# Token rows permuted over the partitions in a fused adaLN, dilated-attention and SwiGLU block

## The chip, the cores and the metric

The kernel runs on one core of a Trainium2 chip. The core has five engines with instruction queues of their own: TensorE (PE, with its weight loads listed as PEld), VectorE (DVE), ScalarE (ACT), GpSimd (POOL) and SyncE (SP), and sixteen DMA engines that all queues share. The metric is the device time of one execution in microseconds (us). A profiled execution gives, beside its time, a trace of every instruction and DMA; the span of that trace is a little shorter than the time.

## The reference

All tensors are bf16; S = 2048 tokens, D = 512, H = 32 heads of 16, F = 1792.

```python
mod = (silu(c) @ w_mod)                  # c is one row; six vectors of D: sa, ca, ga, sb, cb, gb
h = layernorm(x) * (1 + ca) + sa         # LN1
q, k, v = split(h @ wqkv)                # 32 heads of 16
# token s attends to the 8 tokens s, s-2, s-4, ..., s-14 (those >= 0)
logits[s, w] = q[s] . k[s - 2*w] / 4
o[s] = sum_w softmax(logits)[s, w] * v[s - 2*w]
x = x + ga * (o @ wo)
h = layernorm(x) * (1 + cb) + sb         # LN2
x = x + gb * ((silu(h @ w1) * (h @ w3)) @ w2)
```

## The kernel before

The tokens are 16 tiles of 128 rows, one token a partition. Weights and x stay in SBUF.

**LN1 and projections.** Five groups of tiles ([0,1], [2,3], [4..7], [8..11], [12..15]). DVE takes the statistics (L534, L535), POOL the inverse root (L539, L541), DVE normalises (L546). The normalised tile is then turned so that features lie on the partitions: for groups 0 to 2 on PE with an identity matrix (L606), moved out of PSUM by ACT or DVE with the modulation's scale and shift (L614, L621); for the groups named in `DMA_T[0]` (3 and 4) by a DMA transpose that SP issues, and ACT scales in place (L591). PE projects q and k with features on the partitions (L661), which ACT evicts to `q` and `kT` (L670, L671), and v with tokens on the partitions (L681), which ACT evicts (L691) and SP stores to a scratch buffer in DRAM, `v_scratch`. That buffer has 16 zero rows in front.

**Attention, tile by tile.** DVE multiplies q with eight shifted copies of k in one instruction (L712). PE sums each head's 16 features with a block matrix E (L722): 16 matmuls of 256 columns with a 128x32 stationary operand, in four column groups that run side by side; tile 0 gets a mask first (L719). DVE takes the maximum, subtracts (L734, L739), ACT takes the exponential for two tiles (L752), DVE sums, inverts, scales (L764, L766, L767), PE turns the weights so that (token, shift) pairs lie on the partitions (L777), and ACT evicts them (L781). The values arrive from `v_scratch` in that layout: the partition is a pair (one of 16 token runs, shift w), and the free dimension is eight tokens of 512 features. Before the change this is four DMAs a tile, each with 2 KB runs (two consecutive tokens):

```python
for q in range(4):
    p.dma(vv[:, 2*q:2*q+2, :], AP(v_dram, (PAD + T*P + 32*q)*D, [[2*D, 16], [-DIL*D, W], [1, 2*D]]), ...)
```

DVE multiplies weights and values (L797), PE sums over the shifts with an indicator (L825), ACT evicts (L831), a DMA transpose turns the result, PE applies `wo` (L837), which DVE has scaled by ga, and DVE adds to x (L841).

**LN2 and FFN.** Six groups ([0,1], [2,3], [4..7], [8..11], [12,13], [14,15]). POOL and ACT normalise (L556, L560, L567, L571), the tile is turned on PE (groups 0 and 1) or by DMA (`DMA_T[1]`), and for 14 feature blocks PE computes gate and up (L853), ACT the SiLU (L859), DVE the product (L862). PE applies w2 (L891; in halves for tiles 14 and 15, L879), DVE adds x (L901), and SP stores.

**What sets the order.** The program is a list of operations with a cost, read and write sets, and buffer slots. Two written lists, `ORDER` (one position for each operation) and `SLOTS` (buffer numbers), come from a search against a cost model, in which `packet_ns` and the constants in `Program.dma` price the DMAs. Each engine runs its operations strictly in the order of that list and waits on semaphores, so a waiting instruction holds everything behind it on its engine; SP's queue holds nearly all DMA issues. `GATES` adds waits in front of some weight loads.

Of the kernel before, what the change touches and what calls it, by code (L numbers as in the profile page):

```python
# [10 lines left out]
P = 128  # L11
# [58 lines left out]
def packet_ns(size):  # L70
    return {256: 18, 512: 27, 768: 36, 1024: 48, 2048: 92, 3072: 138}[size]


class Program:
# [41 lines left out]
    def dma(self, out, in_, key, packets, r=(), w=(), part=(), after=(), eng="sp", cost=450, group=None, transpose=False,  # L116
            store=False, again=False, lat=None):
        nc = self.nc

        def fn(e):  # L120
            a = out() if callable(out) else out
            b = in_() if callable(in_) else in_
            with nc.allow_non_contiguous_dma(reason="layout"):
                return e.dma_start(a, b, transpose=True) if transpose else e.dma_start(a, b)  # L124

        n, size = packets
        each = -(-n // 16)
        ns = 600 if transpose else each * (126 if again else packet_ns(size))
        o = self.op(eng, fn, cost, key, r=r, w=w, part=part, after=after, dma=(each, ns, *(lat if lat else (900, 200) if store else (900, 500) if transpose else (1300, 600))))
        if group is not None:  # L130
            group.append(o)
            o.group = group
        return o
# [116 lines left out]
BEFORE = -1e9 / P  # L250
# [17 lines left out]
DMA_T = ((3, 4), (2, 3, 4, 5))  # L268
AC_OLD = ()
# [3 lines left out]
def _build(p, A_x, A_wqkv, A_wo, B_w1, B_w3, B_w2, c, w_mod, out):  # L273
# [4 lines left out]
    x_view = x2d.rearrange("(t p) d -> p t d", p=P)  # L278
# [26 lines left out]
    ident = sb([P, P], bf, "ident")  # L305
    E_sb = sb([P, KT, H], bf, "E")
# [53 lines left out]
    def held(pool, items):  # L360

        vals = []
        for i, item in enumerate(items):
# [13 lines left out]
                                           pattern=[[-1, P]], channel_multiplier=1), 300, k, w=[vident])  # L377
    p.op("pool", lambda e: e.memset(cst[:, 0:1], EPS), 80, k, part=[vcst])
# [13 lines left out]
    for y in range(2):  # L392
        p.op("dve", lambda e, y=y: e.tensor_copy(bass.AP(ind2, 33 * y, [[64, P], [2, 16]]), ind[:]), 150, k, r=[vind], w=[vind2])
    p.op("pool", lambda e: e.memset(before[:], 0.0), 250, k, w=[vbefore])
    p.op("pool", lambda e: e.affine_select(out=before[:], in_=before[:], compare_op=ALU.is_ge, fill=BEFORE, base=0,
                                           pattern=[[-DIL, W], [1, 2], [2, 16]], channel_multiplier=0), 400, k, w=[vbefore])
# [10 lines left out]
    p.dma(x_sb[:, 0:2, :], x_view[:, 0:2, :], ("load", 1), (256, 1024), w=vx[0:2])  # L407
    p.dma(wm_s[0][:], wm_view[:, :, 0:1024], ("load", 2), (512, 2048), w=[vwms[0]])
    p.dma(x_sb[:, 2:4, :], x_view[:, 2:4, :], ("load", 27), (256, 1024), w=vx[2:4])
# [4 lines left out]
    for g in range(1, 4):  # L414
        p.dma(x_sb[:, 4 * g:4 * g + 4, :], x_view[:, 4 * g:4 * g + 4, :], ("load", 5 + g), (512, 1024), w=vx[4 * g:4 * g + 4])
# [163 lines left out]
    def ln_T(which, gi, vns):  # L579
        vh = Val("h", hpool)  # L580
        vh.pieces = [Val(f"h_{ft}") for ft in range(KT)] if not which and not gi else None
# [15 lines left out]
        for half in range(2):  # L597
            k = ("tr", (2 * gi + half) + (2 * len(LN1) if which else 0))
            vt = Val("ps_tr", psum)
            for tt in range(n):  # L600
                def tr(e, tt=tt, vt=vt, half=half):
                    b = bank(vt).bitcast(bf)
                    for j in range(2):
                        col = j * 512 + tt * P
                        ft = 2 * half + j
                        ins = e.transpose(b[:, col:col + P], vns[tt].at[:, ft * P:(ft + 1) * P], ident[:])  # L606
                    return ins

                p.op("pe", tr, 114, k, r=[vns[tt], vident], part=[vt])
# [35 lines left out]
    def proj_qk(gi, Ts, kind, vh):  # L645
# [7 lines left out]
        for f0 in range(0, KT, m):  # L653
# [13 lines left out]
            def ev(e, f0=f0, vp=vp):  # L667
                src = bank(vp)[:, 0:m * n].rearrange("p (j n) -> p j n", j=m)
# [4 lines left out]
            p.op("act", ev, c_act(m * n), k, r=[vp], part=[dstv])  # L673

    def proj_v(T, tt, vh):
# [19 lines left out]
        p.dma(v_dram[PAD + T * P:PAD + (T + 1) * P, :], lambda: vt.at[:], k, (128, 1024), r=[vt], w=[vd], cost=400, store=True)  # L695
# [5 lines left out]
    def logits(Ts):  # L701

        vl = Val("ps_l", psum)
        for i, T in enumerate(Ts):
# [11 lines left out]
            def red(e, i=i, T=T, vp=vp):  # L716
                c0 = vl.at * 512 + i * W * 32
                if T == 0:
                    e.matmul(PALL[0:32, c0:c0 + W * 32], ones[:, 0:32], before[:], start=True, stop=False, tile_position=(0, 0))  # L719
                for ft in range(KT):  # L720
                    for q in range(4):
                        ins = e.matmul(PALL[32 * q:32 * q + 32, c0:c0 + W * 32], E_sb[:, ft, :], bass.AP(vp.at, ft * P + 32 * q, [[W * KT * P, P], [KT * P, W], [1, 2], [2, 16]]),  # L722
                                       start=(ft == 0 and (T > 0 or q > 0)), stop=(ft == KT - 1), tile_position=(0, 32 * q))
# [61 lines left out]
    def values(T, i, val):  # L785

        vv = Val("vsh", vshpool)
        loads = []
        for q in range(4):
            p.dma(lambda q=q: vv.at[:, 2 * q:2 * q + 2, :],  # L790
                  bass.AP(v_dram, (PAD + T * P + 32 * q) * D, [[2 * D, 16], [-DIL * D, W], [1, 2 * D]]), ("vl", T), (128, 2048),
                  r=[vv_dram[T]] + ([vv_dram[T - 1]] if T else [vvpad]), part=[vv], group=loads, cost=640, again=True)
# [10 lines left out]
        if T in AC_OLD:  # L803
            def acc(e):
                b = bank(vo)
                for g in range(8):
                    for ft in range(KT):
                        ins = e.matmul(b[:, ft * P + 16 * g:ft * P + 16 * g + 16], vv.at[:, g, ft * P:(ft + 1) * P], ind[:],
                                       start=True, stop=True)
                return ins  # L810

            p.op("pe", acc, C_ACC, ("ac", T), r=[vv, vind], w=[vo])
    
            def ev(e):
                dst = bass.AP(vt.at, 0, [[KT * P, P], [32, 4 * KT], [1, 2], [2, 16]])
                src = bass.AP(PALL, bank(vo).offset, [[8 * 512, P], [32, 4 * KT], [16, 2], [1, 16]])
                return e.activation(dst, src, ACT.Copy)

            p.op("act", ev, c_act(512), ("ac", T), r=[vo], w=[vt])
        else:  # L820
            def acc2(e):
                c0 = vo.at * 512
                for y in range(2):
                    for q in range(4):
                        ins = e.matmul(PALL[32 * q:32 * q + 32, c0:c0 + 512], ind2[:, y, :], vv.at[:, 2 * q + y, :], start=(y == 0),  # L825
                                       stop=(y == 1), tile_position=(0, 32 * q))
                return ins

            p.op("pe", acc2, C_RED, ("ac", T), r=[vv, vind2], w=[vo], tiled=True)
            va = Val("ac", acpool)  # L830
            p.op("act", lambda e: e.activation(va.at[:], bank(vo), ACT.Copy), c_act(512), ("ac", T), r=[vo], w=[va])  # L831
            p.dma(lambda: vt.at[:], lambda: va.at[:], ("ot", T), (128, 1024), r=[va], w=[vt], cost=1270, transpose=True)
# [66 lines left out]
    def store(T, c0, n, vz):  # L899
# [3 lines left out]
        finals.append(p.dma(out2d[T * P:(T + 1) * P, c0:c0 + n], lambda: vo.at[:, 0:n], ("zo", T), (128, 2 * n), r=[vo], cost=400, store=True))  # L903
# [47 lines left out]
GATES = [-1, -1, -1, -1, -1, -1, -1, -1, -1, 1, -1, -1, -1, -1, -1, 1, -1, -1, 2, -1]  # L951
ORDER = [
    19, 18, 5, 0, 1, 3, 8, 55, 20, 14, 64, 15, 22, 67, 4, 2, 21, 66, 9, 65, 26, 58, 10, 23, 56, 24, 62, 50, 25, 85, 60, 29, 57, 86, 51,
    27, 61, 16, 87, 52, 88, 80, 63, 53, 59, 34, 81, 89, 28, 54, 82, 91, 83, 68, 84, 95, 70, 69, 74, 72, 75, 94, 36, 90, 77, 96, 93, 73,
    71, 113, 97, 103, 92, 133, 123, 152, 79, 138, 78, 153, 128, 150, 108, 76, 144, 151, 190, 154, 155, 191, 182, 129, 139, 124, 109,
    183, 180, 145, 104, 134, 114, 125, 181, 105, 11, 157, 140, 110, 156, 146, 135, 188, 184, 115, 185, 126, 147, 111, 127, 189, 141,
    192, 148, 106, 130, 186, 136, 163, 162, 142, 187, 116, 131, 159, 193, 158, 107, 143, 340, 112, 6, 164, 149, 98, 99, 194, 100, 118,
    37, 165, 101, 341, 119, 195, 120, 121, 35, 161, 17, 198, 199, 197, 236, 204, 160, 203, 202, 196, 205, 137, 237, 172, 246, 122, 117,
    206, 247, 168, 290, 200, 291, 342, 238, 173, 170, 207, 239, 298, 240, 166, 241, 379, 102, 299, 244, 132, 7, 171, 174, 32, 245, 201,
    243, 12, 248, 177, 253, 242, 169, 296, 249, 167, 348, 297, 250, 224, 368, 349, 300, 251, 369, 358, 212, 255, 220, 213, 254, 222,  # L960
    356, 216, 223, 252, 178, 210, 225, 46, 343, 359, 288, 301, 371, 217, 357, 289, 303, 175, 179, 214, 302, 380, 211, 360, 292, 293,
    378, 230, 258, 361, 176, 259, 295, 350, 226, 294, 233, 370, 390, 215, 362, 345, 307, 256, 208, 351, 381, 363, 227, 209, 31, 364, 33,
    257, 218, 365, 228, 262, 388, 231, 229, 30, 366, 285, 263, 232, 367, 306, 270, 221, 372, 219, 260, 305, 279, 261, 304, 286, 13, 266,
    382, 271, 280, 47, 268, 287, 267, 373, 234, 389, 346, 344, 400, 374, 383, 391, 375, 384, 420, 272, 309, 235, 276, 310, 281, 401,
    311, 282, 347, 392, 385, 308, 264, 393, 277, 402, 316, 422, 269, 265, 403, 274, 283, 413, 394, 376, 411, 395, 410, 421, 396, 423,
    412, 397, 386, 39, 377, 278, 398, 41, 320, 387, 399, 284, 275, 611, 334, 404, 613, 331, 317, 612, 324, 321, 424, 614, 405, 273, 615,
# [79 lines left out]
```

## Time and profile before

| | us |
|---|---|
| three runs | 245.97, 275.12, 1143.53 (median 275.12) |
| profiled execution, its time | 243.86 |
| profiled execution, its span | 242.0 |
| PE busy | 232.3 |
| DVE busy | 180.0 |
| ACT busy | 135.6 |
| POOL busy | 23.2 |
| mean share of the 16 DMA engines (queue q1) | 61.6% |

The three runs lie far apart, and the profiled execution is close to the lowest of them. TensorE ran at full granted clock throughout. The costliest groups by line are the gate and up matmuls (L853, 102.7 us), the w2 matmuls (L891, 43.3), the q and k projections (L661, 31.6) on PE, and the query-key and weight-value products (L712, 36.4; L797, 29.7 and 6.9 for two names of the buffer) on DVE. The DMA issues of the page by number: 64 V loads of 256 KB (names sb_vsh and sb_vshx), 36 transposes, 18 output stores, 16 V stores, 20 late weight loads, five loads of x.

In such a page, a row of a stage or a group gives busy time and how many instructions; "idle before" is the time that the engine stood still in front of them and what ended it. A chain of waits is followed back from the last instruction, at each step to what released it.

### The profile page before, as it was taken

How to read it: one execution, taken by the hardware profiler on the slowest of the kernel's cores; microseconds unless marked ns; L12 is line 12 of the kernel's file. 1: busy time of each engine (PE TensorE's matmuls, PEld its weight loads, DVE VectorE, ACT ScalarE, POOL GpSimd, SP SyncE). 2: the span in 40 equal slices, each digit the busy share in tenths (PEclk: the TensorE clock that was granted, in tenths of full speed). 3: DMA queues.
4: the chain of work that ended last, by engine and by line, in shares of the span. 5: the costliest groups of instructions: out<-in, count | busy, mean ns of one | idle time of the engine just before them, and what ended most of it. 6: DMA issues, size and time to landing. Idle time of an engine off the chain costs nothing.

```text
span 242.0 us, 4516 instructions
## 1 busy us (share of the span) xinstructions
PE 232.3 (96%) x1778; PEld 135.8 (56%) x1803; DVE 180.0 (74%) x278; ACT 135.6 (56%) x269; POOL 23.2 (10%) x66
## 2 busy tenths in 40 slices
PE   7999999979899999999999999999999999999995
PEld 2667454434368777674444454444444555768864
DVE  4689999968899999999999999928443611433532
ACT  2178498757979743794774479262476334314200
POOL 4144110002003000040000012000010100000000
PEclk9999999999999999999999999999999999999999
DMA  6998999899999879698292189674031010010004
GB/s 219 385 355 286 172 257 264 132 253 261 305 323 285 228 199 237 148 270 176 71 242 80 33 172 240 141 174 131 3 103 27 0 24 22 23 45 0 3 0 130
DMA packets 45756, 38.84 MB, mean 160 GB/s; under 512 B 21656, under 2 KB 36520, under 8 KB 45736
## 3 DMA queue, kind: packets, MB, share of 16 engines
q1 hardware_dynamic: 45728, 38.56, 61.6%
q8 instruction: 14, 0.23, 0.4%
q14 instruction: 6, 0.05, 0.1%
q10 hardware_dynamic: 8, 0.00, 0.0%
HBM read 29.62 MB, written 4.21 MB: 140 GB/s over the span
## 4 chain that ended last, share of the span: by engine, by line
PE 73%; DVE 13%; DMA 6%; SPq 3%; ACT 1%; issue 1%; POOL 0%; DVEq 0%; ACTq 0%
PE pall L853 39%; PE pall L891 17%; DVE sb_pq L712 5%; PE pall L837 4%; DMA sb_vsh<-v_scratch_dram 3%; SPq L124 3%; PE pall L825 2%; PE pall L497 2%; PE pall L879 2%; DVE sb_vsh L797 2%; DVE sb_st L534 2%; DMA sb_wo<-in_A_wo_dram 2%; DMA v_scratch_dram<-sb_v 2%; PE pall L722 2%; PE pall L661 1%
## 5 line engine op out<-in xcount | busy, mean ns | idle before, releaser
L853 PE MATMUL pall<-sb_h,sb_w 128*128 128x256 bf16 (+1 forms) x665 | 102.7, 307 | 0.9 <-ACT sb_sg L859 0.4
L853 PEld LDWEIGHTS pall<-sb_h,sb_w 128*128 128x128 bf16 x672 | 64.6, 98 | 36.0 <-issue 1.3
L859 ACT ACTIVATE sb_sg<-pall 128x256 bf16<-128x256 f32 (+1 forms) x84 | 35.1, 455 | 49.1 <-PE pall L853 44.4
L862 DVE TENSOR_TENSOR sb_hh<-sb_sg,pall 128x256 bf16<-128x256 bf16 (+1 forms) x84 | 39.6, 506 | 29.0 <-PE pall L853 27.1
L891 PE MATMUL pall<-sb_w,sb_hh 128*128 128x512 bf16 x187 | 43.3, 379 | 0.5
L712 DVE TENSOR_TENSOR sb_pq<-sb_q,sb_kT 128x4096 bf16<-128x4096 bf16 x16 | 36.4, 2285 | 0.0
L661 PE MATMUL pall<-sb_h,sb_wqkv 128*128 128x512 bf16 (+1 forms) x156 | 31.6, 335 | 1.6 <-ACT sb_h L591 0.7
L797 DVE TENSOR_TENSOR sb_vsh<-sb_vsh,sb_al 128x4096 bf16<-128x4096 bf16 x13 | 29.7, 2288 | 3.2 <-DMA sb_vsh<-v_scratch_dram 1.9
L891 PEld LDWEIGHTS pall<-sb_w,sb_hh 128*128 128x128 bf16 x196 | 19.0, 98 | 20.7 <-issue 0.4
L591 ACT ACTIVATE sb_h<-sb_h,sb_modc 128x512 bf16<-128x512 bf16 (+1 forms) x24 | 16.4, 737 | 15.7 <-DMA sb_h<-sb_xn 15.6
L661 PEld LDWEIGHTS pall<-sb_h,sb_wqkv 128*128 128x128 bf16 x160 | 14.7, 98 | 13.6 <-ACT sb_h L591 1.3
L901 DVE TENSOR_TENSOR sb_o<-pall,sb_x 128x512 bf16<-128x512 f32 (+1 forms) x18 | 11.1, 628 | 14.4 <-PE pall L891 11.7
L681 PE MATMUL pall<-sb_wqkv,sb_h 128*128 128x512 bf16 x63 | 16.5, 379 | 0.1
L837 PE MATMUL pall<-sb_wo,sb_ot 128*128 128x512 bf16 x61 | 15.6, 379 | 1.0 <-DMA sb_ot<-sb_ac 0.8
L556 POOL TENSOR_SCALAR sb_nm<-sb_sx 128x2 f32<-128x2 f32 x8 | 2.7, 332 | 129.0 <-DVE sb_x L841 129.0
L614 ACT ACTIVATE sb_h<-pall,sb_modc 128x256 bf16<-128x256 bf16 (+1 forms) x18 | 10.3, 629 | 7.8 <-PE pall L606 7.8
L831 ACT ACTIVATE sb_ac<-pall 128x512 bf16<-128x512 f32 x16 | 9.4, 601 | 7.6 <-PE pall L825 7.5
L571 ACT ACTIVATE sb_xn<-sb_x,sb_nb,sb_rs 128x512 bf16<-128x512 bf16 x16 | 12.6, 810 | 1.6 <-POOL sb_nb L569 1.4
L841 DVE SCALAR_TENSOR_TENSOR sb_x<-pall,sb_x 128x512 bf16<-128x512 f32 x16 | 10.7, 686 | 3.6 <-PE pall L837 3.6
L534 DVE BATCH_NORM_STATS2 sb_st<-sb_x 128x6 f32<-128x512 bf16 x16 | 10.7, 669 | 2.2 <-DMA sb_x<-in_A_x_dram 2.2
L671 ACT ACTIVATE sb_kT<-pall 128x512 bf16<-128x512 f32 (+1 forms) x18 | 9.6, 566 | 4.6 <-PE pall L661 4.6
L560 ACT ACTIVATE sb_xn<-sb_x,sb_nm 128x512 bf16<-128x512 bf16 x16 | 11.6, 725 | 0.7 <-POOL sb_nm L556 0.6
(86 smaller groups left out, 202.1 us busy)
## 6 DMA issues: line engine op xcount, KB each, us to landing
sb_vsh<-v_scratch_dram SPq DMA_DIRECT2D x52, 256.0 KB, 4.5
sb_w<-in_B_w_dram SPq DMA_DIRECT2D x6, 512.0 KB, 5.0
sb_vshx<-v_scratch_dram SPq DMA_DIRECT2D x12, 256.0 KB, 5.0
sb_w<-in_B_w_dram SPq DMA_DIRECT2D x6, 384.0 KB, 4.4
v_scratch_dram<-sb_v SPq DMA_DIRECT2D x16, 128.0 KB, 4.1
out_dram<-sb_o SPq DMA_DIRECT2D x14, 128.0 KB, 1.8
sb_wqkv<-in_A_wqkv_dram SPq DMA_DIRECT2D x4, 384.0 KB, 7.7
sb_x<-in_A_x_dram SPq DMA_DIRECT2D x3, 512.0 KB, 7.8
```

Source lines behind the costliest of these rows:

```text
L534: o = p.op("dve", lambda e, T=T: e.bn_stats(st[:, T, :], x_sb[:, T, :]), 595, ("st", T), r=[vx[T]], w=[vs])
L571: p.op("act", lambda e, vn=vn, T=T: e.activation(vn.at[:], x_sb[:, T, :], ACT.Identity, bias=nb[:, T, :], scale=rs[:, NT + T, :]), c_act(5 ...
L591: return e.activation(vh.at[:, ft, 0:n * P], vh.at[:, ft, 0:n * P], ACT.Identity, bias=modc[:, 8 * which + ft:8 * which + ft + 1], scale=m ...
L661: ins = e.matmul(bank(vp)[:, j * n:(j + 1) * n], wqkv[:, t, col:col + P], vh.at[:, t, 0:n], start=(t == ORDER[0]), stop=(t == ORDER[-1]))
L681: ins = e.matmul(bank(vp), vh.at[:, t, tt * P:(tt + 1) * P], wqkv[:, t, 2 * D:3 * D], start=(t == ORDER[0]), stop=(t == ORDER[-1]))
L712: return e.tensor_tensor(vp.at[:], in0, in1, ALU.mult)
L797: return e.tensor_tensor(v_w, v_w, a_w, ALU.mult)
L837: ins = e.matmul(bank(vy), vt.at[:, ft, :], wo[:, ft, :], start=(ft == 0), stop=(ft == KT - 1))
L853: ins = e.matmul(bank(vp)[:, 0:n], wt[:, t, fi * P:(fi + 1) * P], vh.at[:, t, 0:n], start=(t == 0), stop=(t == KT - 1))
L859: p.op("act", lambda e: e.activation(vt.at[:, 0:n], bank(vgp)[:, 0:n], ACT.Silu), c_act(n), k, r=[vgp], w=[vt], table="silu")
L862: p.op("dve", lambda e: e.tensor_tensor(vh_.at[:, 0:n], vt.at[:, 0:n], bank(vup)[:, 0:n], ALU.mult), c_dve(n), k, r=[vt, vup], w=[vh_])
L891: ins = e.matmul(bank(vz), vhh[fi].at[:, tt * P:(tt + 1) * P], w2[:, fi, :], start=(fi == 0), stop=(fi == NF - 1))
```

## The change

Partition p of a tile holds another token than before: token row g + 8x of the tile lies on partition 16g + x (g from 0 to 7, x from 0 to 15). The loads of x and the stores of the output go through a row pattern with that order; x is loaded tile by tile, 15 loads on SP's queue and one (tile 1) on ACT's.

```diff
-    x_view = x2d.rearrange("(t p) d -> p t d", p=P)
+    def rows(t, T, c0=0, w=D):
+        return bass.AP(t.tensor, t.offset + T * P * D + c0, [[D, 8], [8 * D, 16], [1, w]])
...
-    p.dma(x_sb[:, 0:2, :], x_view[:, 0:2, :], ("load", 1), (256, 1024), w=vx[0:2])
+    def load_x(T, eng="sp"):
+        p.dma(x_sb[:, T, :], rows(x2d, T), ("load", 40 + T), (128, 1024), w=[vx[T]], eng=eng)
+    load_x(0)
+    load_x(1, "act")
...
-        finals.append(p.dma(out2d[T * P:(T + 1) * P, c0:c0 + n], lambda: vo.at[:, 0:n], ("zo", T), (128, 2 * n), r=[vo], cost=400, store=True))
+        finals.append(p.dma(rows(out2d, T, c0, n), lambda: vo.at[:, 0:n], ("zo", T), (128, 2 * n), r=[vo], cost=400, store=True))
```

q, k and the scratch buffer of v keep the tokens' natural order. Where LN1 turns a tile on PE, a permutation matrix (two new POOL operations) takes the identity's place. Where a DMA turns it (`vh.turned`, groups 3 and 4), the evictions of q and k write in permuted columns, and the V store goes through the row pattern.

```diff
+                        ins = e.transpose(b[:, col:col + P], vns[tt].at[:, ft * P:(ft + 1) * P],
+                                          ident[:] if which else perm[:].rearrange("p x g -> p (x g)"))
...
+                if vh.turned:
+                    src = bass.AP(PALL, bank(vp).offset, [[8 * 512, P], [P, n // P], [16, 8], [1, 16]])
+                    to = [[P, n // P], [1, 8], [8, 16]]
+                    if kind == 0:
+                        return e.activation(bass.AP(dstv.at, f0 * 512 + at0, [[KT * 512, P]] + to), src, ACT.Copy, scale=SCALE)
+                    return e.activation(bass.AP(kT, f0 * (PAD + S) + PAD + 512 * cch + at0, [[KT * (PAD + S), P]] + to), src, ACT.Copy)
...
+        p.dma(bass.AP(v_dram, (PAD + T * P) * D, [[D, 8], [8 * D, 16], [1, D]]) if vh.turned else v_dram[PAD + T * P:PAD + (T + 1) * P, :], ...)
```

The logit reduction picks its tokens in steps of eight (16 bytes) instead of two (4 bytes), so that the eight tokens of a partition in the V layout are consecutive rows of the scratch buffer, and V is one load of 1 MB with 8 KB runs a tile. The mask of tile 0 becomes four matmuls with one contraction row each.

```diff
-                    e.matmul(PALL[0:32, c0:c0 + W * 32], ones[:, 0:32], before[:], start=True, stop=False, tile_position=(0, 0))
+                    for q in range(4):
+                        e.matmul(PALL[32 * q:32 * q + 32, c0:c0 + W * 32], ones[32 * q:32 * q + 1, 0:32], before[32 * q:32 * q + 1], start=True,
+                                 stop=False, tile_position=(32 * q, 32 * q))
...
-  bass.AP(vp.at, ft * P + 32 * q, [[W * KT * P, P], [KT * P, W], [1, 2], [2, 16]])
+  bass.AP(vp.at, ft * P + 2 * q, [[W * KT * P, P], [KT * P, W], [1, 2], [8, 16]])
...
-        for q in range(4):
-            p.dma(lambda q=q: vv.at[:, 2 * q:2 * q + 2, :],
-                  bass.AP(v_dram, (PAD + T * P + 32 * q) * D, [[2 * D, 16], [-DIL * D, W], [1, 2 * D]]), ("vl", T), (128, 2048),
+        p.dma(lambda: vv.at[:], bass.AP(v_dram, (PAD + T * P) * D, [[8 * D, 16], [-DIL * D, W], [1, 8 * D]]), ("vl", T), (128, 8192),
```

LN2's group 1 (tiles 2 and 3) is turned by DMA instead of on PE. The cost model's DMA constants change, and `ORDER`, `SLOTS` and `GATES` are replaced by the result of a new search; an unused branch (`AC_OLD`) goes.

```diff
-DMA_T = ((3, 4), (2, 3, 4, 5))
-AC_OLD = ()
+DMA_T = ((3, 4), (1, 2, 3, 4, 5))
...
-    return {256: 18, 512: 27, 768: 36, 1024: 48, 2048: 92, 3072: 138}[size]
+    return {256: 18, 512: 27, 768: 36, 1024: 47, 2048: 92, 3072: 127}[size]
...
-        ns = 600 if transpose else each * (126 if again else packet_ns(size))
+        ns = 650 if transpose else each * (400 if again else packet_ns(size))
```

In the new order SP's queue begins x0, x2, w_mod's first half, wqkv (third block), x3, x5, two blocks of wqkv, x4, the last block, x7, x6, the two gate parts of w_mod, x9, x8, the zero rows, x10, x11, part of wo, two V stores, x12, x15, x14. On DVE the statistics of tiles 13 and 12 follow the first two query-key products instead of those of tile 12 alone. At the end, w2 pieces of tiles 15 and 14 come ahead of the second w2 halves of tiles 12 and 13.

## The prediction

> **What bounds the kernel now.** First the summary page: TensorE (PE) is busy 96% of the span at full clock, so the most that can be won is its idle time. Then the same by stage (busy time of each engine per stretch), cut near the first query-key product (25), where PE begins to idle (45), and near the first SiLU (73).
>
> ```profile
> PE 232.3 (96%) x1778; PEld 135.8 (56%) x1803; DVE 180.0 (74%) x278; ACT 135.6 (56%) x269; POOL 23.2 (10%) x66
> ...
> q10 hardware_dynamic: 8, 0.00, 0.0%
> ```
> ```profile
> 0.00:25.00 25.00, 22.50 (x204) 14.46 (x207) 18.29 (x59) 12.47 (x26) 10.07 (x32) 1.00 0.93 305
> 25.00:45.00 20.00, 19.79 (x193) 10.12 (x193) 19.86 (x21) 16.20 (x30) 1.03 (x3) 1.00 0.98 213
> 45.00:73.00 28.00, 25.20 (x207) 12.79 (x204) 23.86 (x28) 21.54 (x40) 2.18 (x5) 1.00 1.06 275
> 73.00:240.00 167.00, 164.82 (x1186) 98.47 (x1201) 118.00 (x173) 85.39 (x175) 9.96 (x28) 1.00 0.46 115
> ```
>
> After the stretch come PE, PEld, DVE, ACT, POOL, the clock, the DMA share and GB/s. PE idles 2.5 us before 25, 0.2 to 45, 2.8 to 73, and 2.2 in the 167 us after. Up to 73 the 16 DMA engines are full (0.93 to 1.06); behind it they are half empty. So 45 to 73 is the stage in question. What PE lacks there is told by the chain of waits in that window and by who VectorE (DVE) waited for:
>
> ```profile
> 41.43 2.20 DVE sb_vsh L797
> 43.63 1.34 SPq L124
> ...
> 45.65 3.87 DMA v_scratch_dram<-sb_v
> ...
> 53.74 0.60 SPq L124
> ...
> 54.38 6.96 DMA sb_vsh<-v_scratch_dram
> ...
> 61.37 2.29 DVE sb_vsh L797
> ```
> ```profile
> DVE sb_ssum L764 <- ACT pall L752: 2.0, 1, 2.0
> ...
> DVE sb_vsh L797 <- DMA sb_vsh<-v_scratch_dram: 1.9, 2, 1.1
> ```
>
> Between two attention products (L797) the chain is SP issuing DMAs, a V store landing, SP again, and a V load of 6.96 us. On DVE's timeline the first L712 starts at 24.84, and the L739 that frees the last exponential before the FFN ends at 71.32: 46.5 us, of which 2.0 + 1.9 = 3.9 are the two waits above, so 42.6 of work. That exponential, a table load, and the first SiLU at 73.24 follow; from there PE is full. The end is the time of this L739 plus a PE-bound remainder, with one hole near the end:
>
> ```profile
> 229.31 1.09 DVE sb_hh L862 x3
> ```
>
> The span is 242.0, the profiled execution 243.86 (1.86 outside the span). The three runs are 245.97, 275.12 and 1143.53; their median is far from anything the trace holds, so I reckon against 243.86, near the lowest.
>
> **The change, part by part.**
>
> V loads: 64 issues of 256 KB become 16 of 1 MB. SP's issue is 593 ns (median of the rows of that tile), so 64 x 0.593 = 38 us of SP become 16 x 0.6 to 1.2 (its longest there) = 10 to 19. Data time: by the queue row q1 moved 38.56 MB in 61.6% of 16 x 242 us, 16.2 bytes/ns per engine; in the first 10 us it moved 2.82 MB in 81.6% of 160 us, 21.6 bytes/ns. A tile is 64 KB per engine: 4.05 us at the mean rate, 3.0 at the better one. So 0 to 1 us less a tile, and none of SP's four-fold queueing: I take 0.5, and of the 3.9 us of DVE waits I let 1.5 remain. The 2.0 us wait at L764 lies behind ACT's in-order queue, which stood still for V stores and transposes; it shrinks with SP's queue but needn't vanish.
>
> x loads: 5 issues become 15 on SP and one on ACT's queue ahead of the c load; 10 x 0.46 = +4.6 us of SP in the first 20, where the queue waits little. The new row pattern has 8 as its outermost DRAM dimension. The nearest row is q10, which carried only the c load, four rows: 8 packets, four of data and four completions, so a transfer with 4 outer rows used four engines. I therefore take eight engines for x, for the permuted V stores and for the output. Price in front: w_mod's first half waits for x0, x1, x2 instead of x0-1. By the rate of 10:20 (3.66 MB in 10 us, so 183 GB/s for eight engines), the eight carry 0.39 + 0.52 = 0.91 MB, 5.0 us, instead of 0.13 + 0.52 = 0.65 MB, 3.6 us: +1.4 on a landing at 6.7, of which PE, at its first modulation matmul at 7.18, feels 0.9. x14 is the last tile DVE needs before its first L712; ahead of it stand 1.97 MB of x and 4.1 MB of other loads and stores, 1.97 + 2.03 = 4.0 MB on the eight, 21.9 us, after a first-byte time of some 2.3 (x0-1: issued 0.79, used 3.69, 0.8 us of data): about 24.5. One statistics pair (0.80) and three normalisations (1.0) later L712 starts at 26.5, against 24.84 now. On sixteen engines x14 would land near 19, and L712 would start when DVE is free: 24.84 less the pair moved behind it (0.80) and less two pairs pulled into waits before 10 us (about 1) = 23.
>
> [...]
>
> One more LN2 group by DMA: PE loses 8 transposes (L606, four in 0.22 us) = 0.44 us, all in the PE-bound part, and 0.6 of PSUM traffic; SP gains two transposes of 1.27. ACT's four moves stay (595 ns from SBUF, 582 from PSUM). They wait for landings of 3.7 us; behind the transposes on SP stand tile 6's V load and the output turns of tiles 5 and 4; behind ACT's moves the SiLUs. Path from the last normalised row: 3.7 + 4 x 0.6 = 6.1 us. Cover: what PE has queued ahead of FFN group 1's first matmul, eight 256-column groups (0.44 each), two weighted sums (0.43) and two w2 halves (1.5), 7.4. I take nothing; with half the cover gone, about 3 us once.
>
> Logit reduction (L722): 16 a tile as before, but its moving operand steps 16 bytes instead of 4. No row shows that step on PE. Lower bound: no change, 0.44 us a tile; upper: the four column groups no longer overlap, 16 x 0.109 = 1.75. ACT's v eviction reads PSUM at 64-byte steps in 605 ns against 601 for a contiguous one, and DVE's L734 reads at 128-byte steps in 686 against 700: steps cost nothing there, so I take 0. Three extra mask matmuls of tile 0 overlap: 0.1.
>
> q and k evictions of groups 3 and 4 (16) write SBUF at 16-byte steps: 606 now, between no change and double; near the strided rows, so 0 to 0.1 each, 1.6 us on ACT, which is idle 10 us between 25 and 73. If doubled, 9.6 us would use that up.
>
> Perm constants, mask, AP of the transposes: same engines, off the path (POOL is 10% busy). Output stores on eight engines: +0.2 at the end.
>
> Order: the DVE list from the first L712 to that L739 holds the same instructions plus one statistics pair, 42.6 + 0.8 = 43.4. At the end, w2 pieces of tiles 15 and 14 now stand between the last up-projections of group 4 and its second w2 half, 1.1 us each: they cover the 1.09 us hole. I allow 0.5 for new holes.
>
> Sum: L739 ends at 26.5 + 43.4 + 1.5 = 71.4 (now 71.32): 0.1. Then -0.44, -1.1, +0.1, +0.2, +0.5: span 241.4, time **243.2**.
>
> **Rivals.**
>
> A, x is not late (sixteen engines, or enough slack): 23 + 43.4 + 1.5 = 67.9, 3.4 earlier; PE can use only its 2.8 of idle time. 241.4 - 0.1 - 2.8 = 238.5, time 240.4; with no DVE wait left and the front 1 us shorter, 239. For it: the c load is tiny, and a 3-dimensional pattern may be dealt out otherwise. Against: the four completions.
>
> B, slower: the reduction pays for its 16-byte step. At twice the time, 0.44 us x 8 tiles behind 73 is 3.5, and the eight before it add 0 to 3.5: 246.7 to 250.2. At the upper bound 1.3 x 16 = 21: 264. It crosses 2% (249) from some 0.8 us a tile. For it: one element per 16 bytes, four streams at once. Against: the strided rows of ACT and DVE.
>
> [...]
>
> C, FFN group 1 starts late behind the DMA transposes: +3, 246.
>
> D, the long load is no faster (mean rate) and the 3.9 us of waits stay: +2.4, 245.6.
>
> **How the numbers follow.** Forecast 0.47, A 0.23, B 0.17, C 0.06, D 0.07. 2% (4.9 us) is about what a measurement of this kernel tells from no change. Faster than 239: half of A and a little of the forecast's low side, 0.17. Slower than 248.7: most of B and a rest of C and D, 0.19. Within: 0.64. The range takes A's lower end and B at twice the time: 238.5 to 250.
>
> **What would show it.** First L712 near 26.5 and a wait of L534 on an x load before it (forecast), or none and about 23 (A); x loads landing late on half the engines. L722's sixteen in 0.44 us (else B). No long SP stretch and no 6.96 us V load in the chain at 45 to 62. PE idle between 45 and 73 near 2. No wait at the last L891. PE waiting at the first matmul of FFN group 1: C. I am wrong if PE's idle time after 73 grows by several us, which nothing here excludes for a reordered queue.

## The result and the profile after

The changed kernel takes 292.2 us (median of 4, 288.97 to 295.03); the kernel before has medians of 243.6 to 245.2 in the comparisons below. Ratios leave out runs that lie far above the others of their kernel (275.12 and 1143.53 of the first runs of before, 295.03 here, 251.31 of the run with all edits below), which would move the medians of the changed kernels by 0.3 us at most. The ratio is 1.1876, 95% interval 1.167 to 1.2082: 47 us slower, where 243.2 had been forecast with 250 as the upper end.

The profiled execution took 288.97 with a span of 287.2. First its summary page: busy time, the granted clock, and the queue that carries the loads of c and of tile 1 of x (packets, MB, share).

```profile
PE 264.7 (92%) x1798; PEld 139.5 (49%) x1798; DVE 181.0 (63%) x278; ACT 162.7 (57%) x269; POOL 25.5 (9%) x68
...
PEclk9669999997699799999999999999999999999999
...
q10 hardware_dynamic: 144, 0.13, 0.1%
```

PE has 32 us more busy time and ACT 27 more for nearly the same instructions. The clock, 1.00 throughout before, falls to 0.50 in four spells (10.2 us from 8.7, 3.4 from 63.3, 6.8 from 70.1, 3.4 from 94.0). q10 had 8 packets for c's four rows, four of 256 bytes and four of 4; now there are 136 more, 128 rows of x and 8 packets of 4 bytes (144 more with natural rows, below, so 16 besides the rows). No view names the engines. Step "x loads" counts one such packet for each engine that a load uses; by that reading, the author's estimate, a tile of x uses eight engines, and with natural rows sixteen. "Eight" and "sixteen engines" stand for these two patterns from here on.

The same by stage (after the stretch PE, PEld, DVE, ACT, POOL, clock, DMA share, GB/s; the first SiLU is now at 104.55):

```profile
0.00:25.00 25.00, 19.33 (x163) 11.79 (x164) 12.60 (x43) 7.16 (x17) 7.52 (x28) 0.80 0.69 228
25.00:45.00 20.00, 20.00 (x126) 9.23 (x125) 16.46 (x29) 13.59 (x26) 3.78 (x8) 1.00 1.06 216
45.00:73.00 28.00, 20.46 (x140) 7.73 (x139) 16.88 (x14) 25.51 (x26) 0.00 (x0) 0.89 0.78 190
73.00:105.00 32.00, 28.42 (x186) 12.12 (x185) 18.02 (x24) 31.97 (x33) 3.13 (x5) 0.88 0.68 186
```

In the first 25 us DVE does 12.6 us of work instead of 18.3 and the DMA engines are no longer full (0.69 against 0.93). From 45 to 105 the full engine is ACT: 25.51 of 28 and 31.97 of 32, while DVE, which had set the pace, works 35 of 60 us. The groups say what ACT and PE do (busy us, mean ns of one, idle before); first the changed kernel, then the same work in the kernel before.

```profile
L743 PE MATMUL pall<-sb_pq,sb_E 128*32 128x256 bf16 x256 | 30.8, 632 | 1.5 <-ACT sb_kT L686 1.5
...
L685 ACT ACTIVATE sb_q<-pall 128x512 bf16<-128x512 f32 x8 | 21.0, 2705 | 0.0
L686 ACT ACTIVATE sb_kT<-pall 128x512 bf16<-128x512 f32 x8 | 20.6, 2663 | 0.0
```
```profile
L671 ACT ACTIVATE sb_kT<-pall 128x512 bf16<-128x512 f32 x14 | 8.2, 606 | 1.1 <-PE pall L661 1.1
...
L722 PE MATMUL pall<-sb_pq,sb_E 128*32 128x256 bf16 x256 | 9.1, 271 | 0.0
```

An eviction of q or k with a 16-byte step takes 2.7 us against 606 ns for the same shape. The reduction's matmuls take 632 ns against 271 (a mean that holds the overlap of four groups; the time that PE needs is the pitch, below). The chain of waits of the changed kernel (start, us, what):

```profile
72.86 2.33 ACT sb_kT L686
75.20 2.28 ACT sb_q L685
77.48 2.29 ACT sb_kT L686
...
149.03 3.78 PE pall L743 x30
...
189.29 10.64 DMA sb_vsh<-v_scratch_dram
```

Where SP, a V store and a V load stood before, there is now one eviction of q or k after another, with ACT's other work between them, until the first SiLU at 104.55. Behind it two tiles of the reduction take 3.78 us, 1.89 a tile; in the reordered run with the old step, below, two take 0.99. Eight tiles lie behind the first SiLU: 8 x 1.4 = 11 of the 14 us by which that remainder grew (182.7 against 168.8 us).

| | first modulation matmul | first query-key product | first SiLU | span |
|---|---|---|---|---|
| before | 7.2 | 24.8 | 73.2 | 242.0 |
| after | 11.3 | 30.4 | 104.5 | 287.2 |

### The profile page after: what moved, and what is told of

It is laid out like the page before. It is cut to its first block, busy times and chain, and to the rows that moved or that the text cites. A ratio compares the mean times of both kernels' runs of the same rounds, so it can differ in the third digit from the quotient of the medians.

```text
span 287.2 us, 4491 instructions
## 1 busy us (share of the span) xinstructions
PE 264.7 (92%) x1798; PEld 139.5 (49%) x1798; DVE 181.0 (63%) x278; ACT 162.7 (57%) x269; POOL 25.5 (9%) x68
## 4 chain that ended last, share of the span: by engine, by line
PE 56%; ACT 23%; DMA 12%; DVE 4%; SPq 2%; issue 1%; ACTq 0%
PE pall L853 29%; PE pall L891 11%; ACT sb_q L685 6%; ACT sb_kT L686 6%; PE pall L743 5%; DMA sb_vsh<-v_scratch_dram 4%; PE pall L837 3%; DMA sb_wm_s<-in_w_mod_dram 3%; DMA v_scratch_dram<-sb_v 3%; DMA sb_ot<-sb_ac 3%; SPq L124 2%; PE pall L825 2%; PE pall L879 2%; ACT sb_h L627 2%; ACT sb_v L710 2%; DVE sb_pq L731 2%
## 5 line engine op out<-in xcount | busy, mean ns | idle before, releaser
L674 PE MATMUL pall<-sb_h,sb_wqkv 128*128 128x512 bf16 (+1 forms) x160 | 34.7, 359 | 4.5 <-ACT sb_h L603 3.6
L743 PE MATMUL pall<-sb_pq,sb_E 128*32 128x256 bf16 x256 | 30.8, 632 | 1.5 <-ACT sb_kT L686 1.5
L815 DVE TENSOR_TENSOR sb_vsh<-sb_vsh,sb_al 128x4096 bf16<-128x4096 bf16 x12 | 27.3, 2287 | 5.1 <-ACT sb_al L802 2.8
L603 ACT ACTIVATE sb_h<-sb_h,sb_modc 128x512 bf16<-128x512 bf16 (+1 forms) x28 | 18.9, 732 | 15.6 <-DMA sb_h<-sb_xn 15.6
L700 PE MATMUL pall<-sb_wqkv,sb_h 128*128 128x512 bf16 x64 | 19.3, 426 | 2.3 <-ACT sb_v L710 1.3
L685 ACT ACTIVATE sb_q<-pall 128x512 bf16<-128x512 f32 x8 | 21.0, 2705 | 0.0
L686 ACT ACTIVATE sb_kT<-pall 128x512 bf16<-128x512 f32 x8 | 20.6, 2663 | 0.0
L755 DVE TENSOR_REDUCE sb_mx<-pall 128x64 f32<-128x512 f32 x8 | 5.5, 691 | 21.8 <-PE pall L743 21.8
L901 DVE TENSOR_TENSOR sb_o<-pall,sb_x 128x512 bf16<-128x512 f32 (+1 forms) x18 | 11.0, 627 | 12.1 <-PE pall L891 10.2
L743 PEld LDWEIGHTS pall<-sb_pq,sb_E 128*32 128x32 bf16 x256 | 7.5, 111 | 19.1 <-issue 16.3
L710 ACT ACTIVATE sb_v<-pall 128x512 bf16<-128x512 f32 x16 | 11.2, 724 | 7.7 <-PE pall L700 5.6
## 6 DMA issues: line engine op xcount, KB each, us to landing
sb_wqkv<-in_A_wqkv_dram SPq DMA_DIRECT2D x4, 384.0 KB, 10.2
```

The source lines that it names most:

```text
L674: ins = e.matmul(bank(vp)[:, j * n:(j + 1) * n], wqkv[:, t, col:col + P], vh.at[:, t, 0:n], start=(t == ORDER[0]), stop=(t == ORDER[-1]))
L685: return e.activation(bass.AP(dstv.at, f0 * 512 + at0, [[KT * 512, P]] + to), src, ACT.Copy, scale=SCALE)
L686: return e.activation(bass.AP(kT, f0 * (PAD + S) + PAD + 512 * cch + at0, [[KT * (PAD + S), P]] + to), src, ACT.Copy)
L700: ins = e.matmul(bank(vp), vh.at[:, t, tt * P:(tt + 1) * P], wqkv[:, t, 2 * D:3 * D], start=(t == ORDER[0]), stop=(t == ORDER[-1]))
L815: return e.tensor_tensor(v_w, v_w, a_w, ALU.mult)
```

## The experiments

**One cost by itself.** A kernel that computes nothing of the reference issues the reduction's sixteen matmuls with other steps of the moving operand, and evictions with other steps of writing and reading.

> This kernel computes nothing of the reference: it runs only matmuls, ACT copies and DVE copies with different steps in their access patterns, and stores zeros. Theory S (a 16-byte step in SBUF is slow by itself): sixteen 256-column matmuls in four column groups take 0.44 us at steps of 2, 4 and 8 bytes and some 1.9 us at 16 bytes, and ACT's 512-element write takes 0.6 us up to 8 bytes and some 2.7 us at 16 bytes, whatever PSUM is read like. Rival L (the four column groups disturb each other by reading the same lines): 16-byte steps are slow only where the groups read the same lines; with each group on lines of its own, or with one 128-column stream alone, 256 columns keep their 0.11 us. Rival R (it is the shape of the pattern, runs of 16 with three dimensions, not the step): a plain one-dimensional 16-byte step is fast.

PE's timeline in that kernel (start, us to the modelled end; the pitch is the difference of starts). The groups have a step of 4 bytes (L122), 16 (L125 as in the change, L128 with each column group in another block), 2 (L131), 4 (L134), 8 (L137), 12 (L140):

```profile
22.08 0.62 PE L122 MATMUL ps<-mov,wt 128*32 128x256 bf16 x16
22.54 2.01 PE L125 MATMUL ps<-mov,wt 128*32 128x256 bf16 x16
24.34 2.03 PE L128 MATMUL ps<-mov,wt 128*32 128x256 bf16 x16
26.18 0.64 PE L131 MATMUL ps<-far,wt 128*32 128x256 bf16 x16
26.63 0.64 PE L134 MATMUL ps<-far,wt 128*32 128x256 bf16 x16
27.09 1.09 PE L137 MATMUL ps<-far,wt 128*32 128x256 bf16 x16
27.98 1.56 PE L140 MATMUL ps<-far,wt 128*32 128x256 bf16 x16
```

Sixteen take 0.46 us at 4 bytes, 0.45 at 2, 0.89 at 8, 1.37 at 12, 1.80 at 16, and hardly more where each group reads another block (1.84; rival L); a plain one-dimensional step of 16 bytes takes 1.80 too (rival R). So PE's time here is the same at 2 and 4 bytes and nearly proportional to the step from there to 16 (in one stream of 128 columns, four matmuls take 1.80 at 16 bytes and 1.84 at 32). Theory S is right on the 16 bytes; the full speed that it expected at 8 bytes isn't there, on PE (0.89 us against 0.46) or on ACT (1302 ns against 597). ScalarE, writing 512 bf16 from PSUM: contiguous (L211), step 16 bytes (L235), the change's own form (L251), and the same elements read in steps from PSUM but written contiguously (L259):

```profile
66.07 0.60 ACT L211 ACTIVATE dstb<-ps 128x512 bf16<-128x512 f32 x1 [64.07 <-PE ps L205]
...
77.00 2.43 ACT L235 ACTIVATE dstb<-ps 128x512 bf16<-128x512 f32 x1
...
96.19 2.43 ACT L251 ACTIVATE dstb<-ps 128x512 bf16<-128x512 f32 x1
...
106.04 0.60 ACT L259 ACTIVATE dstb<-ps 128x512 bf16<-128x512 f32 x1
```

The step of 64 bytes in the PSUM operand (L259) added nothing to ScalarE's 597 ns; with a step of 16 bytes in the SBUF operand (L235, L251) it took 2431 ns, 4.1 times as long.

**The two strides in the kernel.** First the evictions alone: the same elements, stepped in PSUM and contiguous in SBUF.

```diff
-  src [..., [P, n // P], [16, 8], [1, 16]]   to [[P, n // P], [1, 8], [8, 16]]
+  src [..., [P, n // P], [1, 16], [16, 8]]   to [[P, n // P], [8, 16], [1, 8]]
```

> The changed kernel with one edit: the permuted q and k evictions walk their output in order and take the step on the PSUM side. Theory S: L685 and L686 fall from 2.7 us to 0.6 to 0.7 each, 33 us of ACT time, so ACT no longer bounds 45 to 100 us; the first SiLU moves from 104 to about 86 to 90 and the time from 289 to 270 to 275. Rival D (the front and the V loads set the pace of that stage, ACT was busy beside them): the time falls by less than 5 us. Rival R: the eviction stays slow, since the pattern still has three dimensions.

Measured: 278.76 us, ratio 1.1393 (1.1255 to 1.1531); first SiLU at 92.6; an eviction takes 610 ns. Then the reduction alone, with the old 4-byte step, and both:

```diff
-  bass.AP(vp.at, ft * P + 2 * q, [[W * KT * P, P], [KT * P, W], [1, 2], [8, 16]])
+  bass.AP(vp.at, ft * P + 32 * q, [[W * KT * P, P], [KT * P, W], [1, 2], [2, 16]])
```

> The changed kernel with one edit: the logit reduction reads its products in 4-byte steps as before the change, so the attention weights belong to other tokens than they should. Theory S: L743's sixteen matmuls fall from 1.9 us to 0.44 a tile; the eight tiles behind the first SiLU give 8 x 1.45 = 11.6 us, the eight before it little as long as the evictions bound that stage: 289 to about 276. Rival D: less than 5 us.

> The changed kernel with both edits, so the attention weights belong to other tokens than they should. Theory S: what is left over the kernel before is the front (about 5 us: the first projection starts at 14.7 instead of 9.6), the longer V loads and the new order: 250 to 255. If the two prices hide each other, the saving of both is larger than the sum of the single ones. Rival D: above 275.

Measured: 283.64, ratio 1.1593 (1.1483 to 1.1702), and 265.12, ratio 1.0836 (1.0723 to 1.0949); the reduction's matmuls take 278 and 272 ns. Alone the edits win 13.4 and 8.6 us, together 27.1: 5 us more than the sum. The changed kernel's runs spread over 6 us and its profiled executions give 10 instead of 5, so how much each had hidden of the other isn't firm. All three runs are 4 to 10 us above what was expected of them: more than the front is left. With both, the first SiLU is at 84.5, and the page's shares of the chain and its V loads (KB of one, median us to landing) show what is left:

```profile
PE pall L853 28%; DMA sb_vsh<-v_scratch_dram 12%; PE pall L891 10%; DMA sb_h<-sb_xn 6%; PE pall L674 4%; SPq L124 4%; PE pall L837 3%; DMA sb_wm_s<-in_w_mod_dram 3%; DMA sb_ot<-sb_ac 3%; ACT sb_h L603 2%; PE pall L879 2%; PE pall L825 2%; DMA sb_x<-in_A_x_dram 2%; DVE sb_vsh L815 2%; PE pall L700 2%
...
sb_vsh<-v_scratch_dram SPq DMA_DIRECT2D x12, 1024.0 KB, 11.1
```

No eviction of q or k and no reduction is among these; DMA is.

**The DMA parts, on top of both stride edits.** Each V load as four DMAs of 2 KB runs in the new layout; x, V stores and output by natural rows with c ahead of tile 1 of x on ACT's queue; and all of these.

```diff
-  AP(v_dram, (PAD + T*P)*D, [[8*D, 16], [-DIL*D, W], [1, 8*D]])
+  AP(v_dram, (PAD + T*P + 2*q)*D, [[8*D, 16], [-DIL*D, W], [1, 2*D]])   for q in 0..3
...
-  [[D, 8], [8 * D, 16], [1, w]]
+  [[D, P], [1, w]]
```

> a3_both with one edit: each V load is issued as four DMAs of 2 KB runs into the same places of the new layout (the attention weights stay those of other tokens). Theory V (a run of 8 KB is slower per byte than four of 2 KB, and one big load lands late): a run falls from 569 ns for 8 KB to about 120 ns for 2 KB, 1.4 us of data less a tile, the 2.2 us waits of L815 on the load shrink, and the time falls from 265 to 255 to 259 in spite of 48 more issues of 0.6 us on SP. Rival P (the layout is slow: eight consecutive rows, shifted by two rows from one partition to the next): a 2 KB run takes some 142 ns, and the time stays within 3 us of 265. Rival O (SP's issues matter more): slower than 265.

> a3_both with one edit to the DMAs of x, V stores and output: rows in natural order, so that the outermost DRAM size is 128 instead of 8, and c's load ahead of x1 on ACT's queue. Tokens are mixed up by it, and only the time counts. Theory K (eight engines for x hold up w_mod, wqkv and x): w_mod's first half lands 5.5 to 6.5 us after its issue instead of 8.8, SP's issue of an x tile takes 0.46 instead of 0.77, the first projection starts near 10.5 instead of 14.7, PE's clock stays full, and the time falls from 265 to 257 to 260. Rival N (the front's delay comes from 16 small loads and the order, not from the engines): the first projection stays beyond 13, the time within 2 us of 265.

> a3_both with the edits of c1_v_in_2kb_runs and c2_sixteen_engines. If strided reads and writes, eight engines and long runs are all there is to the loss, this is the new order with the old prices: 243 to 250. If it stays above 253, the new order or LN2's third group by DMA has a price of its own.

Measured: 259.55, ratio 1.0555 (1.0451 to 1.0658); 256.27, ratio 1.0421 (1.0265 to 1.0578); both 247.72, ratio 1.0115 (1.0071 to 1.016). Of the 47 us, the strides are 27.1 and the DMA edits 17.4 together; 2.5 remain. The DMA answer of the run with all edits:

```profile
sb_vsh<-v_scratch_dram SPq DMA_DIRECT2D x48, 256.0 KB, 5.7
...
sb_wm_s<-in_w_mod_dram SPq DMA_DIRECT2D x1, 1024.0 KB, 6.0
```

A 256 KB load lands 5.7 us after its issue; with three more issues of 0.6 a tile's V takes some 7.5 (6.3 by the same sum in the kernel before), the single 1 MB load 9.1 to 11.1. The packets explain part of it: in the changed kernel an 8 KB packet took 569 ns on average, in the kernel before one of 2 KB took 120, so if a tile's packets spread evenly over the sixteen engines, eight of 8 KB need 4.55 us on each and thirty-two of 2 KB 3.84 (4.0 to 4.1 in the two runs with 2 KB runs in the new layout, at 125 and 129 ns). Why the single load lands later by more than that isn't shown.

**Engines or c?** The second edit split in two.

> The kernel with both stride edits (contiguous evictions of q and k, 4-byte reduction: attention weights of other tokens), and of the sixteen-engine run's two edits only one: on ACT's queue c is loaded ahead of tile 1 of x. x keeps the eight-row pattern. That kernel without the edit: 265.1 us, tanh of c at 5.3, first modulation matmul at 11.2 (it waits for w_mod's first half), first query-key product at 31.2, first SiLU at 84.5; with both edits 256.3, tanh at 3.1, modulation at 8.7, product at 27.7, SiLU at 79.5. Theory E (the eight engines that carry x make w_mod late): tanh comes at about 3.1 but the modulation still waits for w_mod, so 264 to 266. Rival F (c behind tile 1 of x is what makes the front late): the modulation at about 8.7 and 256 to 258.

> The kernel with both stride edits, and the other of the two edits alone: x, the V stores and the output go by natural rows (outer size 128; tokens are mixed up, as well as the attention weights), c stays behind tile 1 of x on ACT's queue. Theory E: x is spread over sixteen engines, w_mod lands some 2.5 us earlier and the time is 256 to 259. Rival F: tanh of c and with it the modulation stay late, 263 to 265. If half comes from each, 260 to 262.

Measured: c first, 266.31, ratio 1.0884 (1.0821 to 1.0947); natural rows, 256.75, ratio 1.0487 (1.0431 to 1.0543). PE's timeline, first modulation matmul with its wait; c first, then natural rows:

```profile
12.11 0.37 PE L494 MATMUL pall<-sb_csT_bf,sb_wm_s 128*128 128x1 bf16 x8 [4.68 <-DMA sb_wm_s<-in_w_mod_dram]
```
```profile
8.63 0.35 PE L494 MATMUL pall<-sb_csT_bf,sb_wm_s 128*128 128x1 bf16 x8 [1.33 <-DMA sb_wm_s<-in_w_mod_dram]
```

With c first, tanh ran at 3.4 instead of 5.3 and PE waited the longer for w_mod. So theory E held, and the whole 8.4 us go with the row pattern of x, V stores and output: eight engines instead of sixteen, as counted above, and longer issues on SP (1.54 us for the first two x tiles, 0.87 by natural rows). These two weren't separated.

**The clock.** In the changed kernel PE stands idle several times before the modulation (1.9 us before 8.05, 0.8 before 9.35, 1.35 before 11.3), and the granted clock is 0.50 for 10.2 us from 8.7 on (with natural rows, against what was expected of that run, for 6.8 us). More warming matmuls fill the gap (16 with both stride edits; 9 and 18 with natural rows and c first besides).

```diff
-            return e.matmul(bank(vw), ones[:, 0:P], ones[:], start=True, stop=True)
+            for _ in range(16 if i == 6 else 1):
+                ins = e.matmul(bank(vw), ones[:, 0:P], ones[:], start=True, stop=True)
+            return ins
```

> The kernel with both stride edits (attention weights of other tokens), 265.1 us, with nothing moved: the last of the twelve warming matmuls ahead of the modulation is issued 16 times instead of once, so that PE is busy from 7 to about 11 us, where it stood idle and where the granted clock fell to 0.50 for 10.2 us (from 8.3 to 18.6). Theory G (the idle gap takes the clock away, and the half clock costs time of its own): the clock stays at 1.00 over the first 25 us, the first projections run at full speed, and of their 6.6 us of PE work at half clock about 3 are won: first product near 28 to 29, 261 to 263. Rival H (the stage waits for loads anyway, the clock costs nothing): the clock may be full, but the first query-key product stays near 31 and the time is 264 to 266. If the clock drops all the same, the gap is not its cause.

> The kernel with both stride edits, natural rows and c ahead of x1 (tokens mixed up), 256.3 us, with nine more warming matmuls ahead of the modulation, so that PE is busy from 6.5 to about 8.7 us. There the granted clock was 0.50 for 6.8 us; with V in 2 KB runs besides, the front had full clock and the kernel took 247.7, 2.9 us less than the two edits' savings add up to. Theory G: that 2.9 is the clock, so 252 to 254 here with the clock at 1.00. Rival H: no change, 255.5 to 257, and the 2.9 belongs to the V loads that meet an earlier front.

> The kernel with both stride edits, natural rows and c ahead of x1 (tokens mixed up), now with 18 issues of the warming matmul instead of one (nine gave 254.8 us: a gap of 1.05 us remained at 8.4, and the clock was 0.50 for 3.4 us from about 11). PE has no gap before about 10 us. Theory G (with x on sixteen engines PE leads the front, its half clock makes the first V stores late, 18.0 there against 14.6 in the run with full clock): clock 1.00 over the first 25 us, the first V store issued near 15 to 16, first query-key product near 25, 252 to 253.5. Rival H (loads lead the front): V store and product stay at 18 and 27, 254.5 to 256.

Measured: 266.45, ratio 1.0862 (1.0797 to 1.0928); 254.78, 1.041 (1.0354 to 1.0466); 257.72, 1.0556 (1.0489 to 1.0622). PE and the clock in the first, then in the last:

```profile
PEclk9999989899999997999999999997999999999999
...
7.63 3.63 PE L509 MATMUL pall<-sb_ones 128*128 128x512 bf16 x16
```
```profile
PEclk9999999997999997999999999999999999999999
...
10.50 0.34 PE L494 MATMUL pall<-sb_csT_bf,sb_wm_s 128*128 128x1 bf16 x8
```

The gap did take the clock away: filled, the clock is 1.00 over the first 25 us, against 0.80 with both strides undone and nothing filled. With x on eight engines that wins nothing: the first query-key product stayed at 31.7 (31.2 without), and 266.45 stands against 265.12. That stage waits for loads, and the half clock is no price there.

With sixteen engines it is one. From the first modulation matmul to ACT's first V eviction (L710, L712), whose work the first product then waits for, it is 9.1 us at half clock (from 8.74, no filling) and 6.2 at full clock (from 10.50, with 18):

```profile
17.85 0.60 ACT L710 ACTIVATE sb_v<-pall 128x512 bf16<-128x512 f32 x1 [5.46 <-PE pall L700]
```
```profile
16.71 0.60 ACT L712 ACTIVATE sb_v<-pall 128x512 bf16<-128x512 f32 x1 [2.72 <-PE pall L702]
```

But with 18 the filling itself pushed the modulation back by 1.8 us; the product came at 26.5 instead of 27.7, and the time, 257.72, is outside what both theories expected and no better than 256.27. With nine, the 1.5 us lie within the intervals. What a full clock without a later modulation is worth wasn't measured by itself.

## Why the prediction was wrong

- **Reduction: "steps cost nothing there, so I take 0".** This step failed, and the next one with it. The rows it was read from were steps in PSUM, on ACT and DVE; for a moving operand in SBUF they said nothing. The time is 1.8 us a tile against 0.46, slightly above the upper bound of 1.75. Rival B, priced at 264 at that bound, was the right mechanism with a chance of 0.17. Undone alone it gives 8.6 us, undone after the evictions 13.6.
- **Evictions: "0 to 0.1 each", "If doubled, 9.6 us".** 2.7 us instead of 0.6, 4.4 times: (2.684 - 0.606) x 16 = 33 us on ACT, against 10 us of idle time there. "Between no change and double" was no bound, and ACT as the engine that sets the end was no rival: from 45 to the first SiLU the sum let DVE set the pace, and ACT did. Undone alone 13.4 us, after the reduction 18.5. The two strides are 27.1 of the 47 us; they are one error, made in two places.
- **x loads: "eight engines".** Right in kind as far as the packets tell: tile 1's load has 8 packets of 4 bytes, and 16 besides its rows with natural rows. That each stands for one engine is the author's reading, and no run shows the engines themselves. Between eight and sixteen engines the first product moves by 3.8 us (31.2 and 27.4), against 26.5 - 23 in the sum, but that nearness is luck: both ends came over 4 us late. The sum let the product wait for x14 alone, landed at 24.5 or 19 by a count of bytes. But ACT's evictions of q and k wait for projections, and so for the modulation; so do the first two V stores, behind which the last x tiles stand on SP's queue. In the changed kernel and with natural rows the product waits last for an eviction (0.2 us), with both strides undone for x, landed at 28.5. SP in the changed kernel:

```profile
21.18 1.93 SPq L124 DMA_DIRECT2D v_scratch_dram<-sb_v  x2
23.15 1.94 SPq L124 DMA_DIRECT2D sb_x<-in_A_x_dram  x3
```

Too small, too, was w_mod's delay: 0.9 us forecast at the first modulation matmul, 4.1 measured (7.2 to 11.3). One part was left out: two x tiles now took SP 1.54 us to issue, so w_mod was issued at 2.37 instead of 1.31; and its landing then took 8.9 instead of 5.4. But the other eight-engine runs have that matmul at 8.4 to 12.1, and why it varies isn't known; where it came at 8.4 (the reduction alone undone), the product still waited for x until 29.7, so w_mod alone isn't the cause. And where the sum let DVE make up the lateness before the first SiLU (0.1 us), the runs give 8.4 to 8.9 us of time for it (11.8 with V in 2 KB runs).
- **V load: "0 to 1 us less a tile", taken as 0.5.** The sign is wrong: data time 4.55 against 3.84 us an engine, landing 9.1 against some 6.3 from the first issue. The SP time saved is real (16 issues for 64) but was not what the tile waited for. Undone, 5.6 us with eight engines, 8.6 with sixteen. Of the 8.6, 3.3 stand already at the first product (27.7 and 24.4), which waits for no V load: in that run w_mod lands a us earlier, for a reason that isn't known, PE has no gap over 0.3 us before the modulation, and the clock stays full, so that the way from there to the first V eviction is 6.2 us (7.79 to 14.01) instead of 9.1. So the long load's price is between 5 and 9 us, and rival D (2.4) was the right one but too cheap.
- **Order and LN2 group: -0.44 - 1.1 + 0.5.** Together they are no gain: with all four costs undone the new order takes 1.0115 times the time of before, 2.5 to 3 us more, all of it behind the first SiLU (at 72.7; 73.2 before). The hole of 1.09 us at the end is gone, as forecast, but others are new. In the run with all edits: PE's waits from 160 to the end, a piece of its chain, and PE at the first matmul of FFN group 1:

```profile
PE pall L799 <- DVE sb_attn L789: 1.1, 1, 1.1
```
```profile
83.87 9.72 DMA sb_vsh<-v_scratch_dram
```
```profile
90.00 4.98 PE L861 MATMUL pall<-sb_h,sb_w 128*128 128x256 bf16 x44 [0.69 <-ACT sb_h L604]
```

This V load is late (9.72 us, against a median of 5.7) where the DMA engines are full (share 1.15 from 73 to 100, before 0.90): PE idles 6.8 us behind the first SiLU instead of 4.2. The last row is a wait that the LN2 group brings, 0.7 us; what else of this is its 1024 more packets of 256 bytes and what the order wasn't separated.

Rival A's 23 wasn't reached on sixteen engines either (27.4 and 27.7; 24.4 with all edits). Rival C's sign, a wait at the first matmul of FFN group 1, isn't there in the changed kernel; with the strides undone it is, at 1.1 us, and with all edits at 0.7, where the rival had 3. The transposes' landing on that path took 8.3 us with the strides undone, against the 3.7 in the sum, and most of it was covered.

## What to carry to other kernels

A step in an operand has to be priced at the memory it steps through: here rows of strided PSUM reads (605 ns against 601) said nothing of strided SBUF reads by PE (1.80 us against 0.46) and writes by ACT (2431 ns against 597), and where an operand moves from a 4-byte to a 16-byte step, measure it by itself before building a layout on it. When a step must exist, put it on the side that pays nothing (here PSUM: evictions of 610 ns instead of 2.7 us), and undo suspects together as well as alone: two costs in one stage can hide each other (27.1 us together here, 22.0 as the sum of the two, though not firmly). A larger DMA with longer runs is not by itself faster: V as one load of 1 MB landed 9.1 us after its issue, as four of 256 KB in the kernel before some 6.3 after the first (4.5 + 3 x 0.6). And a row pattern whose outermost size is 8 wants a measurement: against natural rows it cost 8.4 us here.

## What the runs showed of the hardware

- TensorE with a bf16 moving operand in SBUF: 0.45, 0.46, 0.89, 1.37, 1.80 us for 16 matmuls of 256 columns at steps of 2, 4, 8, 12, 16 bytes; for four matmuls in one stream of 128 columns, 1.80 at 16 bytes and 1.84 at 32.
- 512 bf16 written from PSUM to SBUF: ScalarE 597 ns contiguous, 737 at 4 bytes, 1302 at 8, 2431 at 16, 2305 at 32; VectorE 690, 726, 1290 and 2419 up to 16. ScalarE writing f32 at 16 bytes, 1066. Reading SBUF at a 16-byte step and writing contiguously took less: 1102 on ScalarE, 614 on VectorE (294 contiguous).
- In the changed kernel the granted clock fell to 0.50 for 10.2, 3.4, 6.8 and 3.4 us. The first of these came where PE had stood idle; with that time filled the clock was 1.00 over the first 25 us (0.80 with nothing filled). With x on eight engines this won nothing (266.45 against 265.12 us); with sixteen it took 2.9 us off the way to the first V eviction.
- 8 KB packets of overlapping runs took 569 ns on average in the changed kernel, four of 2 KB 480 in the kernel before, and 502 and 518 in the new layout.
